# Loading most of w_k in fp32 by the hardware queues, with a newly searched instruction order

## The chip, the cores and the metric

One core of a Trainium2 chip. The metric is the device time of one execution in microseconds (us), as the median of several; lower is better. Two kernels are compared by executions on the same chip, taken in rounds.

## The reference

An attention without softmax, with an RMS norm, feeds a channel-mixing block. There are 8 batches, 8 heads of 64, a sequence of 576, a model width of 512 and a hidden width of 1024.

```python
kv  = einsum('bhsd,bhse->bhde', k, v)
out = einsum('bhsd,bhde->bhse', q, kv)
x   = out / sqrt(mean(out*out) + 1e-6) * g_norm        # then heads are concatenated
xk  = mu_k*x + (1-mu_k)*x_prev ;  xr = mu_r*x + (1-mu_r)*x_prev   # x_prev: one row back
k2  = relu(xk @ w_k) ; r = sigmoid(xr @ w_r)
result = r * ((k2*k2) @ w_v)
```

## The kernel before

The kernel is a set of named pieces (a matmul group, a copy, a load), and one long list, ORDER, says in which order they are emitted. Every engine runs its own pieces in that order, so the list fixes each engine's queue. `qtr0.1` is the transpose of q of batch 0, head pair 1; `kv`, `u`, `ss`, `rr` follow in the attention; `k2.4`, `r2.0`, `v2.0.0` are the matmuls of row group 2 (512 rows); `idle:61` puts 61 filler matmuls on zeros.

```python
def run(self, filler):
    for token in ORDER:
        name, _, eng = token.partition(":")
        if name == "idle":
            filler(int(eng)); continue
        p = self.pieces[name]
        p.fn(eng or p.on[0])
```

Before the change the first head pair of batch 0 comes in fp32 by the SP and ACT queues and is cast on chip. Everything else comes by GpSimd's queue, which casts in flight.

```python
def first_load(n, eng):                      # n in k, v, q
    (nc.sync if eng == "SP" else nc.scalar).dma_start(out=first_view(n), in_=part(n, 0, 0, 2))
...
for i in range(2):                           # w_k in two column halves, cast in flight
    cs = slice(512 * i, 512 * i + 512)
    l = load_w(w_k_sb[:, :, cs], moe_w_k[:, cs], -700 + 0.1 * i, 2.6, f"w_k{i}")
```

From batch 3 on, q is turned by two DMA transposes on SP (`qt6.0` and `qt6.2` in batch 6, one for each two head pairs). A gate on GpSimd reads the first one's result before the next batch is loaded. From batch 5 on the inverse norms make a round trip through DRAM: SP writes them (`ro5`), and two DMAs on GpSimd's queue bring them back, broadcast to 64 partitions each (`rb5`). SP also writes the results (`store...`).

```python
def q_turn(_, hs):
    nc.sync.dma_start_transpose(out=get(qT)[:, hs]..., in_=q2.t[:, hs]...)
...
gate = add({"POOL": 0.3}, lambda _: nc.gpsimd.tensor_copy(out=turned, in_=qT.t[0:1, 0, 0:1]),
           deps=[qtc[0]], bufs=[qT], name=f"gate{b}")
for n in ("k", "v", "q"):
    whole[(n, b + 1)].deps.append(gate)
...
def rms_back(_):
    for e in range(2):
        nc.gpsimd.dma_start(out=get(rs)[64 * e:64 * e + 64],
                            in_=rd.t.rearrange("(i e) c -> e i c", e=2)[e].partition_broadcast(64))
```

Of the kernel before, what the change touches and what calls it, by code (L numbers as in the profile page):

```python
# [15 lines left out]
setup loadq0.2 ident ident9 first_k first_q cast_q:DVE idle:61 qtr0.0 first_v cast_v:DVE cast_k:ACT idle:1 kv0.0  # L16
small qc0.0#2:DVE tr9 qtr0.1 qc0.1#2:DVE qc0.1:DVE qc0.0:ACT edge cols kvc0.0:ACT table u0.0 loadk0.2 loadv0.2 kv0.1
uc0.0:DVE sq0.0 loadq0.6 idle:4 qtr0.3 qc0.3:DVE kvc0.1:ACT u0.1 uc0.1:ACT sq0.1 qc0.3#2:ACT u0.0#2 ss0.0
uc0.0#2:ACT sq0.0#2 gcols rr0.0 mul0.0 d0.0 idle:7 ss0.1 rr0.1 idle:4 ss0.0#2 rr0.0#2 loadq0.4 loadv0.6 loadk0.6
kv0.3 qtr0.2 mul0.1 mul0.0#2 qc0.2#2:ACT kvc0.3:ACT d0.0#2 gk0.0#2:DVE loadv0.4 loadk0.4 idle:6 kv0.2 kvc0.2:ACT  # L20
gk0.1:DVE mr0.1#2:DVE qc0.2:ACT u0.3 uc0.3:ACT sq0.3 idle:7 u0.2 uc0.2:ACT loadq1.0 mt0.0:ACT gk0.0:ACT u0.2#2
uc0.2#2:DVE sq0.2 idle:4 ss0.3 rr0.3 idle:5 ss0.2 rr0.2 sq0.2#2 loadk1.0 loadv1.0 gk0.1#2:DVE idle:1 ss0.2#2 rr0.2#2
xk0.0 d0.1 mr0.1:ACT xk0.1 mul0.3 xk0.1#2 mul0.2 mul0.2#2 gk0.2:DVE gk0.2#2:DVE d0.2#2 idle:11 qtr1.0 qc1.0:ACT
gk0.3:DVE xk0.2 mr0.0:DVE xr0.0 kv1.0 kvc1.0:ACT idle:17 u1.01 u1.00 w_k0 idle:3 k0.a0.1 k0.a0.0 d0.2 xk0.3 k0.a0.2
uc1.01:ACT gk0.3#2:ACT mr0.2:ACT sq1.01 ss1.01 k0.a0.3 rr1.01 relu0.00 xk0.3#2 xk0.2#2 w_k1 idle:6 k0.a1.3 k0.a1.2
uc1.00:DVE d0.3 sq1.00 k0.a1.0 k0.a1.1 relu0.01 ss1.00 mr0.3:DVE xk0.0#2 mr0.2#2:DVE k0.b1 relu0.11 mt0.1:ACT rr1.00
mr0.3#2:DVE ksq0.00 w_r loadv1.4 k0.b0 relu0.10 xr0.2#2 g.w_r:DVE xr0.1 mr0.0#2:DVE mt0.3:DVE xr0.3 xr0.0#2
mt0.2:DVE xr0.2 r0.2 r0.3 sig0.1 g.w_k02:DVE xt0.2 g.w_k12:DVE ksq0.10 loadq1.4 qtr1.2 loadk1.4 qc1.2:DVE kv1.2
kvc1.2:DVE ksq0.11 r0.0 u1.11 uc1.11:ACT u1.10 uc1.10:ACT w_v0 ksq0.01 r0.1 sig0.0 v0.0.0 xt0.0 sq1.11 ss1.11 rr1.11
sq1.10 ss1.10 mul1.0 g.w_k00:DVE v0.2.0 w_v1 v0.2.1 v0.0.1 v0.1.0 v0.3.0 d1.0 xk1.0 rr1.10 mul1.2 d1.2 xk1.2 v0.1.1  # L30
out0.0 store0.0#2 store0.0 g.w_k10:ACT v0.3.1 out0.1 xr1.2 loadq2.0 qtr2.2 qc2.2:ACT qtr2.0 qc2.0:ACT k1.2 k1.3
relu1.1 loadv2.0 loadk2.0 kv2.0 kvc2.0:ACT xr1.0 k1.4 u2.00 u2.11 uc2.11:DVE uc2.00:ACT sq2.00 loadq3.0 ql3.1:DVE
k1.5 relu1.2 u2.01 uc2.01:ACT u2.10 uc2.10:DVE sq2.11 ql3.0:DVE sq2.01 ql3.3:DVE ksq1.1 k1.0 k1.1 relu1.0 ss2.00
rr2.00 k1.6 ss2.01 rr2.01 k1.7 relu1.3 ss2.11 rr2.11 r1.0 ksq1.0 ql3.2:DVE sq2.10 ss2.10 rr2.10 r1.1 sig1.0 r1.2
loadv3.0 loadk3.0 kv3.0 kvc3.0:ACT r1.3 ksq1.2 mul2.0 ksq1.3 v1.0.0 mul2.2 d2.2 xr2.2 qt3.0 u3.00 xk2.2 d2.0 u3.01
uc3.01:ACT sq3.01 uc3.00:ACT sq3.00 sig1.1 xk2.0 qt3.2 v1.0.1 v1.1.0 v1.1.1 out1.0 store1.0#2 xr2.0 ss3.01 rr3.01
ss3.00 rr3.00 v1.2.0 v1.2.1 v1.3.0 v1.3.1 out1.1 gate3 loadq4.0 ql4.2:ACT ql4.0:ACT ql4.1:DVE u3.11 uc3.11:ACT u3.10
mul3.0 uc3.10:ACT ql4.3:DVE k2.4 d3.0 k2.5 relu2.2 ksq2.2 sq3.10 k2.6 k2.7 relu2.3 k2.0 k2.1 relu2.0 sq3.11 ss3.11
ss3.10 rr3.11 k2.2 ksq2.3 rr3.10 mul3.2 k2.3 relu2.1 ksq2.1 r2.0 loadk4.0 loadv4.0 kv4.0 kvc4.0:DVE r2.1 sig2.0
store0.1#2 qt4.0 ksq2.0 u4.01 uc4.01:DVE u4.00 uc4.00:DVE r2.2 r2.3 sig2.1 store0.1 store1.0 xk3.0 sq4.00 qt4.2  # L40
u4.11 uc4.11:DVE u4.10 uc4.10:ACT sq4.10 gate4 loadq5.0 ql5.1:ACT ql5.0:DVE sq4.11 d3.2 xk3.2 v2.2.0 v2.2.1 v2.3.0
ss4.10 ql5.2:ACT v2.0.0 ss4.00 v2.0.1 v2.3.1 out2.1 ql5.3:ACT rr4.10 v2.1.0 ss4.11 xr3.0 v2.1.1 out2.0 rr4.00 rr4.11
mul4.2 k3.0 k3.1 loadv5.0 loadk5.0 kv5.0 relu3.0 kvc5.0:ACT k3.6 xr3.2 qt5.0 gate5 ksq3.0 d4.2 sq4.01 qt5.2 u5.01
u5.00 uc5.01:ACT xk4.2 sq5.01 uc5.00:ACT k3.7 relu3.3 k3.2 u5.11 u5.10 uc5.10:ACT uc5.11:ACT sq5.10 sq5.11 ksq3.3
sq5.00 k3.3 relu3.1 ksq3.1 k3.4 k3.5 relu3.2 ksq3.2 r3.0 ss5 loadq6.0 ql6.2:DVE ql6.3:DVE ql6.0:DVE ql6.1:DVE
store2.1#2 store1.1#2 store2.0 store1.1 rr5 ro5 store2.1 r3.1 ss4.01 rr4.01 mul4.0 d4.0 sig3.0 v3.0.0 v3.0.1 v3.1.0
v3.1.1 out3.0 xr4.0 xk4.0 xr4.2 loadk6.0 loadv6.0 r3.2 r3.3 v3.2.0 v3.2.1 v3.3.0 kv6.0 kvc6.0:DVE v3.3.1 sig3.1
out3.1 k4.4 qt6.0 qt6.2 store3.0#2 store2.0#2 u6.10 u6.01 uc6.01:ACT k4.5 relu4.2 uc6.10:DVE sq6.10 rb5 mul5.0 d5.0
xk5.0 k4.2 k4.3 relu4.1 mul5.2 u6.00 ksq4.2 uc6.00:ACT sq6.00 u6.11 uc6.11:ACT sq6.01 sq6.11 d5.2 xk5.2 ksq4.1 k4.0
k4.1 relu4.0 ksq4.0 r4.0 r4.1 sig4.0 k4.6 ss6 rr6 ro6 gate6 loadk7.0 loadv7.0 kv7.0 loadq7.0 ql7.0:DVE ql7.1:DVE  # L50
qt7.0 store3.0 k4.7 relu4.3 ksq4.3 ql7.3:DVE xr5.2 k5.2 k5.3 ql7.2:ACT relu5.1 rb6 k5.0 k5.1 relu5.0 r4.2 r4.3
v4.2.0 sig4.1 store3.1 v4.2.1 v4.3.0 v4.3.1 store3.1#2 v4.0.0 xr5.0 kvc7.0:DVE u7.01 u7.00 uc7.00:ACT uc7.01:ACT
out4.1 sq7.00 ksq5.1 mul6.0 qt7.2 v4.0.1 v4.1.0 v4.1.1 out4.0 store4.0#2 d6.0 k5.6 k5.7 relu5.3 mul6.2 ksq5.0 sq7.01
u7.11 u7.10 uc7.10:ACT sq7.10 uc7.11:ACT ksq5.3 sq7.11 k5.4 k5.5 relu5.2 ksq5.2 r5.2 r5.3 sig5.1 d6.2 xr6.2 xk6.2
xk6.0 ss7 rr7 store4.1#2 ro7 store4.1 rb7 r5.0 r5.1 v5.0.0 v5.0.1 v5.1.0 v5.1.1 sig5.0 out5.0 store5.0 store5.0#2
store4.0 k6.6 k6.7 relu6.3 k6.2 k6.3 ksq6.3 relu6.1 ksq6.1 xr6.0 k6.0 k6.1 relu6.0 k6.4 k6.5 relu6.2 ksq6.0 mul7.2
ksq6.2 v5.2.0 v5.2.1 v5.3.0 v5.3.1 out5.1 mul7.0 r6.2 r6.3 v6.2.0 sig6.1 v6.2.1 v6.3.0 v6.3.1 d7.0 xr7.0 out6.1 d7.2
xk7.0 store5.1 store6.1#2 store5.1#2 xk7.2 r6.0 r6.1 v6.0.0 v6.0.1 v6.1.0 v6.1.1 sig6.0 out6.0 k8.2 k8.3 relu8.1
ksq8.1 k7.6 k7.7 relu7.3 k8.0 k8.1 relu8.0 ksq8.0 ksq7.3 k8.6 k8.7 relu8.3 k7.0 k7.1 relu7.0 xr7.2 ksq8.3 ksq7.0
k7.4 k7.5 relu7.2 k7.2 k7.3 relu7.1 k8.4 k8.5 relu8.2 ksq7.1 ksq7.2 r7.2 r7.3 v7.2.0 v7.2.1 v7.3.0 v7.3.1 sig7.1  # L60
ksq8.2 out7.1 store6.1 store6.0#2 store7.1#2 store6.0 store7.1 r7.0 r7.1 sig7.0 r8.0 r8.1 sig8.0 v7.0.0 v7.0.1
v7.1.0 v7.1.1 out7.0 v8.0.0 v8.0.1 out8.0 v8.1.0 v8.1.1 out8.0#2 store7.0 store8.0#2 store8.0 store7.0#2 r8.2 r8.3
v8.2.0 sig8.1 v8.2.1 out8.1 store8.1 v8.3.0 v8.3.1 v8.3.0#2 v8.3.1#2 out8.1#2 store8.1#2 out8.1#3 store8.1#3
# [40 lines left out]
def kernel(  # L104
# [125 lines left out]
    first = {n: Buf("out") for n in src}  # L230

    def first_view(n):
        return get(first[n]).rearrange("p a c -> p (a c)")[0:NP, 0:2 * NJ * HD].rearrange("p (h c) -> p h c", h=2)

    def first_load(n, eng):
        def fn(_):
            (nc.sync if eng == "SP" else nc.scalar).dma_start(out=first_view(n), in_=part(n, 0, 0, 2))

        return add({eng: 0.42}, fn, bufs=[first[n]], due=-2000, land=0.8, name="first_" + n)

    firsts = {n: first_load(n, eng) for n, eng in (("k", "SP"), ("v", "ACT"), ("q", "SP"))}
# [31 lines left out]
    def load(b, n, h0, h1, due):  # L273
        def fn(_):
            nc.gpsimd.dma_start(out=get(kvq[(n, b)])[:, h0:h1, :], in_=part(n, b, h0, h1))  # L275

        p = add({"POOL": 0.64 if b == 0 else 0.76}, fn, bufs=[kvq[(n, b)]], due=due, land=(h1 - h0) * (0.37 if b < 3 else 0.43),
                name=f"load{n}{b}.{h0}")
        for h in range(h0, h1):
            loaded[(n, b, h)] = p  # L280
        return p

    whole = {}
    for n in ("k", "v", "q"):
        p = add({"DVE": dve_us(768, 2), "ACT": act_us(768, True)},
                lambda eng, n=n: copy(eng, get(kvq[(n, 0)])[:, 0:2, :], first_view(n)),
                deps=[firsts[n]], bufs=[kvq[(n, 0)], first[n]], name=f"cast_{n}")
        loaded[(n, 0, 0)] = loaded[(n, 0, 1)] = p
    for h0 in (2, 4, 6):
        for i, n in enumerate(("k", "v", "q")):  # L290
            load(0, n, h0, h0 + 2, -900 + 10 * h0 + i)
# [34 lines left out]
    for i in range(2):  # L326
        cs = slice(512 * i, 512 * i + 512)
        l = load_w(w_k_sb[:, :, cs], moe_w_k[:, cs], -700 + 0.1 * i, 2.6, f"w_k{i}")
        p_wk.append([l])
# [627 lines left out]
```

## Time and profile before

| what | before | where |
|---|---|---|
| median time | 203.49 us (203.43 to 204.22) | runs |
| PE busy | 192.6 of 201.7 us, with 12.3 us of fillers | page, parts 1 and 5 |
| second half of k, group 0, starts | 25.12 us | PE timeline |
| PE's listed waits after 35 us | 1.5 us, the largest 0.53 | waits |
| last matmul ends, span ends | 197.5 and 201.7 us | PE timeline |

The prediction below shows the lines. In a timeline line the columns are start, duration, engine, source line, operation, output<-inputs, shapes and count, and in brackets the idle time before it with the name of what ended it. SPq and POOLq stand for what the SP and GpSimd queues issue. Matmul durations in a timeline are modelled ends, so start-to-start times are the safer reading. The granted clock is the share of its full clock that PE was given, as the trace records it.

### The profile page before, as it was taken

How to read it: one execution, taken by the hardware profiler on the slowest of the kernel's cores; microseconds unless marked ns; L12 is line 12 of the kernel's file. 1: busy time of each engine (PE TensorE's matmuls, PEld its weight loads, DVE VectorE, ACT ScalarE, POOL GpSimd, SP SyncE). 2: the span in 40 equal slices, each digit the busy share in tenths (PEclk: the TensorE clock that was granted, in tenths of full speed). 3: DMA queues.
4: the chain of work that ended last, by engine and by line, in shares of the span. 5: the costliest groups of instructions: out<-in, count | busy, mean ns of one | idle time of the engine just before them, and what ended most of it. 6: DMA issues, size and time to landing. Idle time of an engine off the chain costs nothing.

```text
span 201.7 us, 4116 instructions
## 1 busy us (share of the span) xinstructions
PE 192.6 (95%) x1629; PEld 103.4 (51%) x1651; DVE 147.2 (73%) x332; ACT 116.2 (58%) x148; POOL 33.4 (17%) x53
## 2 busy tenths in 40 slices
PE   7999899999999999999999989999999999999991
PEld 7867775454544454543457654444444444444451
DVE  1589988998898959799799985699486854432321
ACT  2588688666978597948723887268452226644020
POOL 7964314000050040040053010000200000000000
PEclk9999999999999999999999999999999999999998
DMA  6999999999969999999999949530742240003263
GB/s 173 200 202 207 204 205 205 204 203 248 171 100 200 217 217 193 173 207 216 207 251 248 203 70 231 156 104 5 185 143 51 66 132 15 2 0 101 69 193 108
DMA packets 39976, 31.69 MB, mean 157 GB/s; under 512 B 13812, under 2 KB 35092, under 8 KB 39956
## 3 DMA queue, kind: packets, MB, share of 16 engines
q0 software_dynamic: 21504, 18.11, 57.0%
q1 hardware_dynamic: 17780, 12.42, 25.9%
q10 hardware_dynamic: 672, 0.89, 1.3%
q8 instruction: 13, 0.21, 0.4%
q14 instruction: 7, 0.06, 0.1%
HBM read 35.33 MB, written 9.46 MB: 222 GB/s over the span
## 4 chain that ended last, share of the span: by engine, by line
PE 74%; DMA 13%; POOL 4%; ACT 3%; issue 2%; SPq 1%; DVE 0%; DVEq 0%; POOLq 0%; ACTq 0%
PE mm L795 25%; PE mm L875 24%; PE mm L853 12%; DMA w_k<-in_moe_w_k_dram 5%; DMA v<-in_v_dram 5%; DMA qT<-q 3%; PE at L649 2%; PE at L567 2%; PE mm L522 2%; PE mm L815 2%; PE mm L892 2%; PE at L892 2%; PE at L701 2%; POOL k L275 1%; POOL q L275 1%
## 5 line engine op out<-in xcount | busy, mean ns | idle before, releaser
L795 PE MATMUL mm<-xk,w_k 128*128 128x512 bf16 (+1 forms) x281 | 58.5, 355 | 0.4
L875 PE MATMUL mm<-w_v,sqk 128*128 128x512 bf16 x251 | 57.8, 379 | 0.6 <-issue 0.3
L799 ACT ACTIVATE relu<-mm 128x1024 bf16<-128x1024 f32 x36 | 36.9, 1024 | 27.1 <-PE mm L795 23.2
L795 PEld LDWEIGHTS <-w_k 128*128 128x128 bf16 x288 | 27.2, 98 | 26.7 <-issue 1.8
L875 PEld LDWEIGHTS <-sqk 128*128 128x128 bf16 x256 | 24.7, 98 | 29.2 <-issue 1.1
L853 PE MATMUL mm<-w_r,xr 128*128 128x512 bf16 x135 | 33.4, 379 | 0.8 <-issue 0.5
L879 DVE TENSOR_TENSOR out<-mm,sig 128x1024 f32<-128x1024 f32 x16 | 19.5, 1223 | 19.8 <-PE mm L875 15.8
L858 ACT ACTIVATE sig<-mm 128x1024 bf16<-128x1024 f32 x18 | 18.4, 1025 | 26.6 <-PE mm L853 26.5
L802 DVE TENSOR_TENSOR sqk<-relu 128x1024 bf16<-128x1024 bf16 x32 | 21.7, 687 | 10.9 <-ACT relu L799 10.7
L853 PEld LDWEIGHTS <-xr 128*128 128x128 bf16 x144 | 13.5, 98 | 15.6 <-issue 0.9
L185 ACT CAST uT<-at 128x576 bf16<-128x576 f32 x21 | 12.6, 641 | 12.2 <-PE at L649 12.2
L743 DVE TENSOR_SCALAR md<-d,cols 128x576 bf16<-128x576 bf16 x56 | 18.4, 371 | 0.3
L194 ACT ACT_TABLE_LOAD x12 | 15.4, 1283 | 0.2
L763 PE MATMUL mm<-zero 128*128 128x128 bf16 x137 | 12.3, 251 | 1.1 <-DVE zero L245 1.1
L717 DVE TENSOR_TENSOR xT<-uT,rs 128x1152 bf16<-128x1152 bf16 x14 | 10.5, 752 | 2.9 <-ACT rs L705 2.8
L656 DVE TENSOR_TENSOR sq<-uT 128x576 bf16<-128x576 bf16 x28 | 12.1, 451 | 0.8 <-ACT uT L185 0.6
L705 ACT ACTIVATE rs<-at,eps 128x576 bf16<-128x576 f32 x16 | 11.2, 738 | 1.8 <-PE at L701 1.7
L763 PEld LDWEIGHTS <-zero 128*128 128x128 bf16 x137 | 10.5, 116 | 2.9 <-issue 1.3
L684 POOL DMA_DIRECT2D rs<-rd x6 | 3.8, 634 | 44.2 <-DVE xk L746 20.6
L746 DVE TENSOR_TENSOR xk<-md,xT 128x1152 bf16<-128x1152 bf16 x14 | 10.6, 759 | 0.5
L746 DVE TENSOR_TENSOR xr<-md,xT 128x1152 bf16<-128x1152 bf16 x14 | 10.6, 759 | 0.5
L729 DVE TENSOR_TENSOR d<-xT 128x1152 bf16<-128x1152 bf16 x14 | 10.5, 753 | 0.2
(89 smaller groups left out, 175.2 us busy)
## 6 DMA issues: line engine op xcount, KB each, us to landing
out_dram<-out SPq DMA_DIRECT2D x22, 192.0 KB, 4.7
q<-in_q_dram POOLq DMA_DIRECT2D x6, 576.0 KB, 10.0
v<-in_v_dram POOLq DMA_DIRECT2D x6, 576.0 KB, 12.6
k<-in_k_dram POOLq DMA_DIRECT2D x6, 576.0 KB, 11.1
out_dram<-out SPq DMA_DIRECT2D x23, 128.0 KB, 2.2
rs<-rd POOLq DMA_DIRECT2D x6, 288.0 KB, 5.6
out_dram<-out SPq DMA_DIRECT2D x22, 64.0 KB, 6.6
w_k<-in_moe_w_k_dram POOLq DMA_DIRECT2D x2, 512.0 KB, 11.5
```

The lines of the kernel that those rows point to most:

```text
L185: nc.scalar.copy(out=dst, in_=src)
L194: nc.scalar.preload_act_table_set(name)
L743: nc.vector.tensor_scalar(out=get(md)[:, hp], in0=d.t[:, hp], scalar1=cols[:, m0 + hp:m0 + hp + 1], scalar2=None, op0=ALU.mult)
L746: nc.vector.tensor_tensor(out=dst[:, hs, c0:c0 + S], in0=md.t[:, hs], in1=xT.t[:, hs, 0:S], op=ALU.add)
L763: nc.tensor.matmul(get(k_ps[i])[:, 0, 0:128], zero[:, 0:128], zero[:, 128:256], start=not k_seen[i], stop=not k_seen[i])
L795: nc.tensor.matmul(get(ps)[:, fc % 2, a0:a1], w_k_sb[:, cc, 128 * fc:128 * fc + 128], xk[:, cc, x0:x0 + a1 - a0], start=(cc == 0), stop=(c ...
L799: nc.scalar.activation(out=get(rt), in_=ps.t, func=AF.Relu)
L802: nc.vector.tensor_mul(out=get(sqk)[:, 2 * f2:2 * f2 + 2, :], in0=rt.t, in1=rt.t)
L853: nc.tensor.matmul(get(ps)[:, ci % 2, :], xr[:, cc, n0:n0 + 128], w_r_sb[:, cc, :], start=(cc == 0), stop=(cc == NHP - 1))
L858: nc.scalar.activation(out=get(sg), in_=ps.t, func=AF.Sigmoid)
L875: nc.tensor.matmul(get(ps)[:, ci % 2, :], sqk.t[:, fc, 128 * ci:128 * ci + 128], w_v_sb[:, fc, :], start=(fc == 0), stop=(fc == NFC - 1))
L879: nc.vector.tensor_mul(out=get(ot)[:, xs, :], in0=ps.t[:, xs, :], in1=sg.t[:, xs, :])
```

## The change

The intent is to have w_k on chip before PE wants it. Three of its four row blocks (512 KB each in fp32) take the fast first place on the SP and ACT queues and are cast on chip. The first head pair goes to GpSimd's queue like the others, and the fourth row block stays there. The order was searched again, all of it, with two of the search's landing estimates raised.

```diff
-    first = {n: Buf("out") for n in src}
+    first = [Buf("out") for _ in range(3)]
-            (nc.sync if eng == "SP" else nc.scalar).dma_start(out=first_view(n), in_=part(n, 0, 0, 2))
+            (nc.sync if eng == "SP" else nc.scalar).dma_start(out=first_view(i), in_=moe_w_k[128 * i:128 * i + 128, :])
-    for h0 in (2, 4, 6):
+    for h0 in (0, 2, 4, 6):
         for i, n in enumerate(("k", "v", "q")):
             load(0, n, h0, h0 + 2, -900 + 10 * h0 + i)
+    p_wk = [add(..., lambda eng, i=i: copy(eng, w_k_sb[:, i, :], first_view(i)), ..., name=f"cast_{i}") for i in range(3)]
+    p_wk.append(add({"POOL": 0.8}, lambda _: nc.gpsimd.dma_start(out=w_k_sb[:, 3, :], in_=moe_w_k[384:512, :]), ...))
-    land=(h1 - h0) * (0.37 if b < 3 else 0.43)
+    land=(h1 - h0) * (0.37 if b < 3 else 0.45)
-    rms_back, deps=[c], bufs=[rd, rs], land=2.2
+    rms_back, deps=[c], bufs=[rd, rs], land=3.2
     ...                      # ORDER: every line differs; the place that matters later:
-    ro5 store2.1 ... qt6.0 qt6.2 store3.0#2 ... rb5 mul5.0
+    ro5 ... store2.0#2 qt6.0 store2.0 qt6.2 ... rb5 mul5.2
```

## The prediction

> **What bounds the kernel now.** I read the page from the top, then the chain that ended last in order of time, then PE's own timeline of the first 26 us, then a table of DMA share by stretches of 1 us, and last PE's waits after 35 us.
>
> ```profile
> span 201.7 us, 4116 instructions
> ...
> PE 192.6 (95%) x1629; PEld 103.4 (51%) x1651; DVE 147.2 (73%) x332; ACT 116.2 (58%) x148; POOL 33.4 (17%) x53
> ...
> PE 74%; DMA 13%; POOL 4%; ACT 3%; issue 2%; SPq 1%; DVE 0%; DVEq 0%; POOLq 0%; ACTq 0%
> ...
> L763 PE MATMUL mm<-zero 128*128 128x128 bf16 x137 | 12.3, 251 | 1.1 <-DVE zero L245 1.1
> ```
>
> PE is the bound, but not all of its 192.6 us is work: the 137 matmuls on L763 are fillers on zeros, which stand where PE has nothing to do in the prologue. After about 25 us PE is dense: its listed waits after 35 us add up to 1.5 us, the largest being 0.53 us for a v load at 116.5 us. So the end is, to about 1 us, the moment when the dense work starts, plus a fixed 172 us of matmuls, plus the last stores (last matmul at about 197.6, end at 201.7). The change acts on the moment when the dense work starts, and the rest is a reordering.
>
> ```profile
> 1.06 5.91 PE L763 MATMUL mm<-zero 128*128 128x128 bf16 x61 [1.06 <-DVE zero L245]
> 6.89 0.45 PE L387 MATMUL a<-ident,q 96*64 96x96 bf16 x12
> ...
> 20.80 1.49 PE L522 MATMUL mm<-xk,w_k 128*128 128x256 bf16 x12 [0.59 <-DMA w_k<-in_moe_w_k_dram]
> ...
> 25.12 1.15 PE L815 MATMUL mm<-xk,w_k 128*128 128x256 bf16 x9
> ```
>
> Fillers run to 6.89 us, when the first q pair has come (fp32) and is cast. L522 is the first half of k of group 0: it waits for w_k until 20.80, though its other input, xk of the first head pairs, is there from about 16.8 us (the first fused multiply ends then). L815, the second half, opens the dense part at about 25.0 us (the weight load says 25.00). This is the wait that the change is after: the chain has 10.92 us of "DMA w_k" from 9.83 to 20.75.
>
> ```profile
> 3.00:4.00 1.00, 1.00 (x12) 1.00 (x10) 0.00 (x0) 0.00 (x0) 1.00 (x3) 1.00 1.07 352
> 4.00:5.00 1.00, 1.00 (x13) 1.00 (x11) 0.00 (x0) 0.15 (x1) 1.00 (x3) 1.00 1.11 263
> ...
> 7.00:8.00 1.00, 1.00 (x27) 0.83 (x26) 0.49 (x2) 0.33 (x1) 0.97 (x2) 1.00 1.31 199
> ```
>
> The last two columns are DMA share and GB/s. At 3 to 4 us only the fp32 loads (SP and ACT queues) run: 352 GB/s. From 5 us on it is the casting loads: 199 to 204 GB/s until 44 us, counted at the bf16 destination, so some 400 GB/s of fp32 source. The DMA is full all through the prologue: what comes first decides everything.
>
> **What the Trainium skill says.** "DMA: Bandwidth & Descriptors", section "SWDGE vs HWDGE vs iDMA": a cast in flight needs the GpSimd path, the other queues only copy, both kinds run on the same 16 engines, which take turns between them. The trace agrees on the first (every load with a cast is on POOL); that the two take turns I must assume for the new overlap, as before they hardly overlap. The same page, "Latency and other measured facts", gives a first byte after 0.6 us (HWDGE) and about 1 us (SWDGE). Here the first SWDGE load is issued at 1.30 us, yet the rate falls from 352 to 263 only at 4 to 5 us and to 208 at 5 to 6: some 3 us. The measurement decides, and it leaves the engines open to fp32 loads for that long. "VectorE: DVE Perf Modes", "The perf-mode tier table", puts an fp32 copy in SBUF at twice the base rate; here the DVE cast of 96x768 takes 556 to 572 ns, which fits (768/2/0.96 = 400 ns, plus a fixed part). "TensorE: Matmul & The Clock Gate", "Wait — 56ns, not 53.3ns?": 128-column matmuls stand 107 ns apart cold and 56 warm. Here the first 61 fillers stand 5.83/61 = 96 ns apart, later ones 55 to 64 (17 in 1.08 us).
>
> **The change part by part.**
>
> *Removed:* three fp32 loads of head pair 0 (3 x 288 KB = 0.88 MB), their casts (ACT 0.83, DVE 0.56 and 0.57 us), and the two casting loads of w_k (2 x 512 KB at the destination).
>
> *Added:* three fp32 loads of 512 KB (1.57 MB), three casts of 128x1024 (from the measured 768-column ones: one DVE, about 0.70 us, two ACT, about 1.05 us each), three more casting loads for head pair 0 (147 kB at the destination each) and one for the last w_k block (262 kB). The scaling of w_k by g, four pieces as before, goes from three on DVE (478 ns) and one on ACT (1147 ns) to one and three: DVE minus 0.96, ACT plus 2.3 us, at 35 to 40 us, where ACT is busy 3.6 of 5 us. Hidden.
>
> *Fillers:* 137 become 133, but 83 instead of 61 stand first. 83 x 96 ns = 7.9, so the first transposes come at about 9.0 us instead of 6.89. The other 50 at 57 ns make 2.85 us. In all 10.8 us against 5.83 + 76 x 0.057 = 10.2: plus 0.6 us of filler.
>
> *When things land.* The fp32 loads have the engines alone from 1.3 to about 4.4 us: some 0.9 MB at up to 352 GB/s. The other 0.67 MB share. If packets alternate, 4 KB fp32 against 768 B casting (4096 B at 352/16 GB/s is 186 ns, the other 79 ns), fp32 gets about 250 GB/s and is in at about 7 us, with 125 kB of casting loads beside it. From there casting bytes run at 200 GB/s. Completion trails the running sum, in the kernel before, by about 0.8 us early and 1.5 us late (w_k0 and w_k1 there: sums give 18.6 and 21.2, landings 20.75 and 22.7). So, sum and lag together: q of the first pair 8.1, its k and v 9.5; head pair 0 11.9; all of batch 0 16.7 (before: 12.6); first half of batch 1 21.3; the last w_k block 22.8; w_r 26.6; w_v 32.2 and 34.8. The last three are as before: 5.38 MB of casting bytes behind 1.57 MB of fp32, against 5.72 behind 0.88, end at 33.4 against 33.5. The DMA total is no gain.
>
> *PE to the dense part.* The matmuls before L815 are the same but for the two sums of squares of batch 1, 0.24 us each, which move behind it. Non-filler work by start-to-start times is about 10.9 us before and 10.4 after. With 1.06 at the start and the fillers, 22.2 us before (25.0 measured, so 2.8 of waits) and 22.3 after, plus its waits. What it must wait for: the last w_k block at 22.8, then 0.44 each for the last block's two pieces, 0.37 for u of batch 1, 0.44 for the last piece: 24.5 us. By the other path, batch 0 complete at 16.7, kv, u, copy, square, sum, rsqrt, multiply, blend (0.38+0.2+0.85+0.36+0.3+0.6+0.42+0.3, then 0.9 for the other multiply and 0.48) give the last head pair's xk at 21.9, and six more DVE pieces before the second halves are ready: 24.7. So L815 starts at about 24.7 instead of 25.0, 0.3 us earlier, and pays 0.48 us for the two moved sums: plus 0.2 us.
>
> *Later.* The one large wait, 0.53 us at 116.5 (v of batch 7), follows a gate, two stores in front of the transposes on SP (0.51 and 0.59 us in the chain) and a load of 10.54 us. The new order puts more PE work in front of that kv, so I count minus 0.5. A longer assumed landing for the broadcast of the norms and for the loads says that the search now plans with slower DMA, so I take another minus 0.2 for small waits. Sum: 203.5 + 0.2 - 0.5 - 0.2 = 203.0.
>
> **Rivals.**
>
> *Freed w_k:* if w_k was the only brake, xk being ready at 16.8, then 20.8 - 17 = 3.8 us is to be had, time about 199.7. Against: head pairs now come 2 to 4 us later, the fillers are not fewer in time, and the last w_k block still comes by the slow path at 22.8.
>
> *Turned wait:* head pair 1 starves beside the fp32 loads, batch 0 lands 2 us later than I think, and DVE, busy 5.00 of 5.00 us at 15 to 20 already, becomes the path into L815. Time about 205. For it: DVE's share. Against: the casts cost DVE 0.4 us less than before.
>
> *Nothing but the new order:* the prologue is a wash and only the schedule's luck counts, 202.5 to 204. Close to my own view.
>
> **Range and chances.** PE's 172 us of dense work doesn't change, so 2% (4.07 us) would need all of the first rival. I put 203.0, with 201.5 to 204.9 for eight in ten: below, some 40% of what the first rival would bring (1.5 of 3.8 us); above, a prologue later by 1.9 us, nearly the second rival. Faster by 2%: 0.03; slower by 2%: 0.03.
>
> **What would show it.** First transposes at 8.5 to 9.5 us; k0's first matmuls (L522's successor) between 17 and 19 us without a wait for w_k; a wait of PE for the last w_k block, or for xk, at 21 to 23; the second half starting at 24.2 to 25.2; fewer than 1.5 us of listed waits after 35 us. I am wrong if the second half starts before 23.5 (first rival) or after 26 (second), or if PE after 45 us is longer or shorter by more than 1 us.

## The result, and the profile after

The changed kernel took 209.41 us in the median (208.37, 208.78, 210.04 and 211.78) against 203.49. The ratio of its fast runs to the fast runs of before is 1.0266, with a 95% interval of 1.0205 to 1.0326. A ratio here is the mean of one kernel's fast runs over the mean of the other's in the same rounds, so not quite the ratio of the medians. Executions over 1.5% slower than the fastest of the same kernel are left out of the means. The profiled execution was the slowest one, 211.78 us, 1.6% above the fastest, and so it counts as a slow run. I use it for the mechanism. Its sum below accounts for that one execution and is not the size of the change; the size is the ratio of the fast runs, some 5.4 us. The two fastest runs, 208.37 and 208.78 us, had a mean granted clock of 0.992 against 0.979, so they lost less to the clock.

The page after, busy time and chain by engine, and the granted clock by slice of 5.2 us:

```profile
span 209.9 us, 4114 instructions
...
PE 196.1 (93%) x1626; PEld 104.5 (50%) x1647; DVE 148.0 (70%) x326; ACT 116.3 (55%) x151; POOL 34.1 (16%) x55
...
PEclk9999999999999999999997699999999999999998
...
PE 56%; DMA 33%; POOL 2%; issue 2%; SPq 2%; ACT 2%; DVE 1%; POOLq 0%; ACTq 0%
```

The span is 8.2 us longer, PE's share of the chain has fallen from 74% to 56%, and DMA's has risen from 13% to 33%. The clock row has a dip in slices 22 and 23, which was not there before.

The start, from PE's timeline of the changed kernel:

```profile
8.40 0.45 PE L384 MATMUL a<-ident,q 96*64 96x96 bf16 x12
...
16.62 0.38 PE L368 MATMUL a<-v,k 96*64 96x64 bf16 x12
...
21.45 0.57 PE L564 MATMUL at<-v,k 96*64 96x64 bf16 x24
...
24.34 1.91 PE L812 MATMUL mm<-xk,w_k 128*128 128x256 bf16 x16
```

The first transposes, the last kv of batch 0, the first kv of batch 1 and the second half of k of group 0 stand at 8.40, 16.62, 21.45 and 24.34 us. The last one was at 25.12 before. So the start is 0.8 us faster, and the loss comes later. PE's waits after 25 us name the places:

```profile
PE at L646 <- DMA qT<-q: 4.1, 1, 4.1
PE at L564 <- DMA v<-in_v_dram: 1.3, 2, 0.9
PE at L564 <- DMA k<-in_k_dram: 0.9, 1, 0.9
```

One wait of 4.1 us, for a transposed q, is larger than all of PE's waits of before together. This is the same stretch of PE's timeline, before (L649 is u, the matmul on qT):

```profile
106.55 1.04 PE L795 MATMUL mm<-xk,w_k 128*128 128x256 bf16 x8
107.59 0.44 PE L649 MATMUL at<-qT,kv 64*64 64x288 bf16 x8
107.96 2.79 PE L795 MATMUL mm<-xk,w_k 128*128 128x256 bf16 x24
```

and after (the same pieces, L792 and L646):

```profile
108.61 1.04 PE L792 MATMUL mm<-xk,w_k 128*128 128x256 bf16 x8
113.73 0.69 PE L646 MATMUL at<-qT,kv 64*64 64x288 bf16 x8 [4.08 <-DMA qT<-q]
114.35 5.14 PE L792 MATMUL mm<-xk,w_k 128*128 128x256 bf16 x24
```

PE stands still for 4.08 us, and then the 24 matmuls that took 2.79 us take 5.14. The table of stretches for the changed kernel shows why; the columns after the length are busy time and count of PE, PEld, DVE, ACT and POOL, then PEclk, DMA share and GB/s:

```profile
110.00:111.00 1.00, 0.00 (x0) 0.00 (x0) 0.96 (x4) 0.00 (x0) 0.00 (x0) 1.00 1.00 104
...
112.00:113.00 1.00, 0.00 (x0) 0.00 (x0) 0.00 (x0) 0.00 (x0) 0.00 (x0) 0.68 1.41 182
113.00:114.00 1.00, 0.27 (x8) 0.18 (x7) 0.00 (x0) 0.00 (x0) 0.00 (x0) 0.50 1.30 198
```

The granted clock falls to one half at about 112.4 us. The trace's clock record holds it there for 6.83 us, to about 119.2, and PE works in 5.5 us of that.

**The account of the profiled execution.** PE's listed waits after 25 us, without "issue" and with the 0.51 us at the tail, come to 6.8 us against 0.7 before. Half of 5.5 us at half clock is 2.7. The start gives back 0.78, less 0.48 (the prediction's estimate) for two sums of squares that moved behind it. The sum is 6.1 + 2.7 - 0.3 = 8.5 us; 211.78 - 203.43 = 8.35 was measured.

Why was the transpose late? SP's queue and GpSimd's queue, before, are:

```profile
97.37 1.15 SPq L774 DMA_DIRECT2D out_dram<-out  x2
98.69 4.72 SPq L603 DMA_TRANSPOSE qT<-q  x2
103.51 2.33 SPq L774 DMA_DIRECT2D out_dram<-out  x4
```

```profile
101.83 1.26 POOL L684 DMA_DIRECT2D rs<-rd  x2 [10.89 <-DMA rd<-rc]
104.16 0.60 POOL L612 COPY turned<-qT 1x1 bf16<-1x1 bf16 x1 [1.07 <-DMA qT<-q]
```

and SP's queue after is:

```profile
99.73 1.54 SPq L600 DMA_TRANSPOSE qT<-q  x1
101.32 1.64 SPq L771 DMA_DIRECT2D out_dram<-out  x2
103.05 2.19 SPq L600 DMA_TRANSPOSE qT<-q  x1
```

and GpSimd's queue after:

```profile
103.21 1.26 POOL L681 DMA_DIRECT2D rs<-rd  x2 [9.59 <-DMA rd<-rc]
```

Before, both transposes of batch 6 go one behind the other. After, a store stands between them, so the second starts to issue at 103.05 us. The broadcast of the norms of batch 5 (`rs<-rd`) is issued at 103.21 us. The chain of the changed kernel has "103.05 10.63 DMA qT<-q": 10.6 us from issue to landing. (Experiment 2 shows the same transpose, issued behind the same store, land in 4.5 us.) The packet records of the two traces (my count, by packet size, in steps of 1 us) show what happened on the engines. A transpose has 1152 packets of 256 B. Before, they ran at 733 and 1018 in a microsecond and were all but done when the 4608 B packets of the broadcast began. After, the first 694 of the second transpose went through within a microsecond. Then the broadcast began, and the rest came at 144, 197, 88 and 29. The 4 B packets, which I take for the reports of the transpose's end, came last, from 111.3 to 112.8 us. The broadcast suffers as well: issue to landing was 5.7 to 6.1 us before and 9.7 to 10.4 after.

Theory A is thus that the new order lets the second transpose run into the broadcast. Theory B is that the gate, which waits for the first transpose alone, lets the loads of batch 7 in beside the second. Theory C is that the new start shifts all later DMA and thereby makes the loss.

### The profile page after: what moved, and what is told of

Same layout as the page of the kernel before. It is cut to its first block, busy times and chain, and to the rows that moved or that the text cites. A ratio compares the mean times of both kernels' runs of the same rounds, so it can differ in the third digit from the quotient of the medians.

```text
span 209.9 us, 4114 instructions
## 1 busy us (share of the span) xinstructions
PE 196.1 (93%) x1626; PEld 104.5 (50%) x1647; DVE 148.0 (70%) x326; ACT 116.3 (55%) x151; POOL 34.1 (16%) x55
## 4 chain that ended last, share of the span: by engine, by line
PE 56%; DMA 33%; POOL 2%; issue 2%; SPq 2%; ACT 2%; DVE 1%; POOLq 0%; ACTq 0%
PE mm L792 19%; PE mm L870 15%; DMA qT<-q 12%; DMA v<-in_v_dram 11%; DMA q<-in_q_dram 10%; PE mm L848 9%; PE mm L519 2%; PE at L887 2%; PE mm L812 2%; PE mm L887 2%; PE at L564 1%; PE at L646 1%; SPq L771 1%; POOL k L276 1%; SPq L600 1%
## 5 line engine op out<-in xcount | busy, mean ns | idle before, releaser
L792 PE MATMUL mm<-xk,w_k 128*128 128x512 bf16 (+1 forms) x282 | 61.1, 367 | 0.4
L792 PEld LDWEIGHTS <-w_k 128*128 128x128 bf16 x288 | 28.6, 102 | 27.9 <-issue 2.0
L853 ACT ACTIVATE sig<-mm 128x1024 bf16<-128x1024 f32 x18 | 18.4, 1023 | 21.3 <-PE mm L848 21.2
L186 ACT CAST uT<-at 128x576 bf16<-128x576 f32 x16 | 9.9, 639 | 12.4 <-PE at L646 12.2
L743 DVE TENSOR_TENSOR xr<-md,xT 128x1152 bf16<-128x1152 bf16 x14 | 10.6, 759 | 0.5
L743 DVE TENSOR_TENSOR xk<-md,xT 128x1152 bf16<-128x1152 bf16 x14 | 10.6, 759 | 0.5
L188 DVE CAST uT<-at 128x576 bf16<-128x576 f32 x12 | 8.9, 753 | 2.9 <-PE at L646 2.8
```

The lines of the kernel that those rows point to most:

```text
L743: nc.vector.tensor_tensor(out=dst[:, hs, c0:c0 + S], in0=md.t[:, hs], in1=xT.t[:, hs, 0:S], op=ALU.add)
L792: nc.tensor.matmul(get(ps)[:, fc % 2, a0:a1], w_k_sb[:, cc, 128 * fc:128 * fc + 128], xk[:, cc, x0:x0 + a1 - a0], start=(cc == 0), stop=(c ...
L853: nc.scalar.activation(out=get(sg), in_=ps.t, func=AF.Sigmoid)
```

## The experiments

All twelve kernels gave correct results. All edits of ORDER are shown by their tokens.

**1. The transposes one behind the other.**

```diff
-store2.0#2 qt6.0 store2.0 qt6.2
+store2.0#2 qt6.0 qt6.2 store2.0
```

> The changed kernel with one pair of tokens swapped on SP: the second transpose of batch 6 directly behind the first, the stores of group 2 (first half) after both. Theory A (the second transpose, issued 3.3 us after the first because two stores stand between, meets the broadcast of the norms of batch 5 on the same DMA engines, and PE waits 4.1 us and then runs at half clock): the wait of PE for qT goes from 4.1 us to under 1 us, and the time from about 208.6 to 203.0-204.8. Theory B (the gate that waits for the first transpose alone lets the loads of batch 7 in beside the second): the gate opens as before, so most of the wait stays, time above 206.5. Theory C (the new start shifts all later DMA): no change, 208-210.

Measured: 203.76, 204.28, 207.39 and 209.84 us, with the kernel before at 203.58 to 205.19. The ratio of the fast runs is 0.9988 (0.9937 to 1.004). In the profiled run (204.28) PE has no wait for qT:

```profile
108.90 0.44 PE L645 MATMUL at<-qT,kv 64*64 64x288 bf16 x8
109.27 2.79 PE L791 MATMUL mm<-xk,w_k 128*128 128x256 bf16 x24
```

The wait and the half clock are gone together: 2.79 us again for the 24 matmuls. One token moved took away the loss in the fast runs, as Theory A said, but only two of the four runs lie in its band. The two runs at 207 and 210 count as slow and have no trace. That the collision came back in them is plausible but not shown: in the profiled run the data of the second transpose was through at 105.7 us, the broadcast began at 105.6, and the 4 B packets at the end came at 107 to 108, with u due at 108.9. The margin was about 1 us.

**2. The broadcast held back.**

```diff
-... k4.3 rb5 mul5.2 ... relu4.0 gate6 loadq7.0
+... k4.3 gate6 rb5 mul5.2 ... relu4.0 loadq7.0
```

> The changed kernel with the gate of batch 6 moved ahead of the broadcast of the norms on the GpSimd queue, so that the broadcast is issued only after the first transpose has landed; the stores still stand between the two transposes. Theory A: the second transpose has 2 to 3 us more of the engines to itself, PE's wait for it falls from 4.1 us to under 2 us, and the time to 203.5-206 (the norms come later and may cost some of it). Theory B: the loads of batch 7 come as early as before, wait and time stay, above 207.5. Theory C: no change.

Measured: 205.25 to 206.79 us, ratio 1.008 (1.0036 to 1.0123). There is no listed wait for qT and the mid-run clock stays full. SP's and GpSimd's queues show the store in its place and the hold:

```profile
102.36 2.25 SPq L599 DMA_TRANSPOSE qT<-q  x1
```

```profile
105.30 0.18 POOL L608 COPY turned<-qT 1x1 bf16<-1x1 bf16 x1 [12.08 <-DMA qT<-q]
105.87 0.65 POOL L680 DMA_DIRECT2D rs<-rd  x1 [0.40 <-issue]
...
107.30 0.79 POOL L275 DMA_DIRECT2D q<-in_q_dram  x1
```

The store still stands between the transposes, the second is issued at 102.36 us, and yet it lands in time, 4.5 us later. The loads of batch 7 are issued at 107.30, near their time in the changed kernel (107.18). So it was the broadcast that the transpose met first; experiment 3 asks about the loads alone. The norms come later, and PE pays 0.6 us for xk and 0.4 for a relu, which it did not before.

**3. The loads of batch 7 held back instead.**

```diff
-tensor_copy(out=turned, in_=qT.t[0:1, 0, 0:1]),                  deps=[qtc[0]]
+tensor_copy(out=turned, in_=qT.t[0:1, 2 if b == 6 else 0, 0:1]), deps=[qtc[2 if b == 6 else 0]]
```

> The changed kernel with the gate of batch 6 waiting for the second transpose in place of the first; order unchanged. Theory A: the loads of batch 7 stand behind the broadcast in the same queue and have moved nothing while the transpose was slow, so PE's wait for qT stays at 3.5 to 4.5 us, and as the loads then come some 5 us later the kv of batch 7 waits too: 208-213. Theory B: the wait falls under 1.5 us and the time to 205 or less. Theory C: no change or worse.

Measured: 208.32, 209.24, 210.88 and 211.35 us, ratio 1.0305 (1.0243 to 1.0368). PE's timeline in the profiled run:

```profile
112.41 0.44 PE L645 MATMUL at<-qT,kv 64*64 64x288 bf16 x8 [3.55 <-DMA qT<-q]
112.78 2.79 PE L791 MATMUL mm<-xk,w_k 128*128 128x256 bf16 x24
```

With the loads out of the way until 112.8 us the wait is still 3.55 us. Theory B falls. This run also gives the wait without the half clock: 208.32 us. Its listed waits (3.5 + 0.9 + 0.5 + 0.4) exceed those of before by 4.6 us, and its time that of the profiled run of before (203.43) by 4.9. Why the clock stayed full here is taken up in the last section.

**4. New loads and start, old order for the rest.** ORDER is the changed kernel's up to `k0.b0`, then the kernel before's list without what has been emitted.

> The changed kernel's loads and its order up to the second half of k of group 0 (about 28 us), and the order of the kernel before for all that is left. Theories A and B (the loss comes from the order after 50 us): 202.7-204.0, within 0.5% of the kernel before. Theory C: the loss stays, above 206.

Measured: 202.79 us once, and 206.41, 206.66 and 206.84. The three count as slow, and one run is left, so there is no ratio. This contradicts what A expected, and three runs lie where C put them. The trace (206.41) shows the same place, though:

```profile
109.50 0.44 PE L645 MATMUL at<-qT,kv 64*64 64x288 bf16 x8 [2.00 <-DMA qT<-q]
109.87 4.46 PE L791 MATMUL mm<-xk,w_k 128*128 128x256 bf16 x24
```

In this order the transposes are adjacent, and they were issued at 98.59 and 100.66 us, as before. On my count their data was through at 105.8 us, just as the broadcast began (105.6), but the 4 B packets that report the end came only at 108.1, when the broadcast was done, and the landing is at 109.5. The collision is thus there in a weaker form, with only the report caught in it: 2.00 us of wait, then 3.41 us at half clock. In this run the start part of the change brings the old order to the edge too. The run at 202.79 lies below all runs of before, but it is a single run and has no trace: what this version is worth without the collision is not shown.

**5. Old start, new order for the rest.** The reverse of 4.

> The kernel before's loads and its order up to the second half of k of group 0, then the changed kernel's order. Theory A (the loss comes with the new order after 50 us, by the second transpose of batch 6 running into the norms' broadcast): PE waits 3 to 4.5 us for qT near 110 us, time 207.5-211. Theory C (the new start, with its other loads, shifts the DMA and thus makes the collision): the wait is under 1 us, time below 205.

Measured: 208.02, 210.87, 211.76 and 213.4 us, ratio 1.027 (1.0177 to 1.0363). The clock halves for 6.83 us, and PE waits for qT as in the changed kernel:

```profile
PE at L649 <- DMA qT<-q: 4.6, 1, 4.6
```

The new order loses by itself, without the new loads, and the ratio is that of the whole change, though two of the runs count as slow and the verdict at 2% is unclear, as the interval begins at 1.0177. Theory C is not needed for the loss.

**6. Both cures.** Experiment 1's swap, and 2's hold with the gate on the second transpose.

> The changed kernel with both cures: the transposes of batch 6 one behind the other, and the broadcast issued only after the gate, which here waits for the second transpose. Theory A: no wait of PE for qT in any execution, so also no run in the 207s and 209s as with the pair alone: all runs 203.0-204.8. If the runs still spread up to 207 and more, something other than this collision makes the slow executions.

Measured: 205.02, 205.43, 205.93 and 206.0 us, ratio 1.0081 (1.0045 to 1.0117). No run reached 207, so the large spread is gone, but the level is 1.2 us above the expected band's upper end at worst. The hold costs more than I thought: PE waits 1.2 us for a v and 0.4 us behind a relu.

**7. Experiment 4 with the hold.**

> New loads and start, the old order for the rest, and the broadcast held until the second transpose has landed. Theory A: the two-valued times of the same kernel without the hold (202.8 once, 206.4 to 206.8 three times) become one value near the lower, 202.5-203.4, about 0.3% under the kernel before. If the 206s stay, the hold was not the cure and the collision not the cause of them.

Measured: 208.52 to 211.39 us, ratio 1.028 (1.0221 to 1.0339). I was wrong. There is no wait for qT any more, but:

```profile
119.35 1.04 PE L667 MATMUL at<-sq,sel 128*32 128x288 bf16 x8 [3.37 <-DVE sq L652]
121.50 1.49 PE L563 MATMUL at<-v,k 96*64 96x64 bf16 x48 [1.11 <-DMA v<-in_v_dram]
```

In the old order the multiply by the norms of batch 5 stands ahead of the squares of batch 6 in DVE's queue. Held norms hold DVE (it sat idle for 4.61 us for them), and PE waits for the squares; behind that the clock halves for 6.83 us. The wait has only moved, so this run is no test of what the collision cost in experiment 4.

**8. The hold alone, on the kernel before.**

> The kernel before with nothing but the hold: the gate of batch 6 waits for the second transpose and stands before the broadcast. Theory A: there the transposes end just as the broadcast starts, so the hold changes little: 203.0-204.0, with less spread. Rival: the hold costs time by itself, as the norms and the loads of batch 7 come later: 204.5-206.

Measured: 204.52 us, and 207.36, 207.46 and 207.53; ratio 1.0137 (1.0064 to 1.0209). The verdict at 2% is unclear, but the rival was right that the hold costs time by itself; three runs lie above even its band, and they have no trace. The hold is evidence about the cause, in 2, and not a cure.

**9. The loads alone.** The changed loads in the order of before, token by token; `w_k1` goes, and the casts stand where the old ones stood.

```diff
-setup loadq0.2 ident ident9 first_k first_q cast_q:DVE idle:61 qtr0.0 first_v cast_v:DVE cast_k:ACT idle:1 kv0.0
+setup loadq0.0 ident ident9 first_0 first_1 idle:61 loadk0.0 loadv0.0 loadq0.2 first_2 cast_1:ACT cast_0:DVE cast_2:ACT qtr0.0 idle:1 kv0.0
```

> The change of the loads alone: three row blocks of w_k by fp32 loads with casts on chip, head pair 0 by casting loads, one casting load for the last w_k block, and otherwise the order of the kernel before, token by token (no new search). My prediction's view (the prologue is a wash): the first transposes come 1.5 to 2.5 us later than before, the second half of k of group 0 starts within 1.2 us of 25.1 us, time 203.5-205.5 if no collision at 105-110 us follows, 206-210 if the small shift brings it about. Rival (the loads free the start): the second half starts before 23.5 us and the time is 202 or less.

Measured: 206.28, 206.6, 208.32 and 209.41 us, ratio 1.0162 (1.0096 to 1.0227), a verdict of unclear at 2%. The second half of k of group 0 starts at 28.68 us, 3.6 us later than before and beyond both expectations. The stretches show what goes with it:

```profile
8.00:10.00 2.00, 1.20 (x26) 1.03 (x27) 0.26 (x1) 0.74 (x3) 1.66 (x3) 0.81 1.31 199
...
14.00:16.00 2.00, 2.00 (x18) 1.56 (x15) 1.31 (x6) 1.75 (x5) 1.02 (x2) 0.50 1.31 198
```

PE waited 1.05 us for the first q at 7.9 and 0.80 us for the first v at 9.35, and the clock was at one half for 6.83 us from 9.25 us on. The times lie in the band that I had given for a collision, but PE's wait for qT is only 0.6 us here: the loss is one of the start. In the changed kernel, with 83 fillers in place of 61, the clock stayed full in the prologue. That the fillers did this is not shown, and experiment 10, with the same start, lost the clock in the prologue all the same.

**10. Experiment 4 with the transposes earlier on SP.**

```diff
-rr5 ro5 store2.1 ... qt6.0 qt6.2 store3.0#2
+rr5 ro5 qt6.0 qt6.2 store2.1 ... store3.0#2
```

> New loads and start, old order for the rest, but the two transposes of batch 6 directly behind the store of the norms on SP, ahead of the store of group 2 that took 1.15 us of SP. Theory A: the transposes are through before the broadcast begins, PE's wait for qT (2.0 us in that order without this) is gone, and the runs fall together near the one good run of it: 202.3-203.3. If they stay at 206-207, the margin is not set by SP.

Measured: 204.51 to 206.51 us, ratio 1.0077 (1.0021 to 1.0134). This sits between the two predictions. In the profiled run SP's norms were written at 98.52 us, 1.9 us later than in 4; the clock had been at one half for 3.41 us in the prologue of that execution, which fits. The transposes were thus issued at 99.62, not earlier, and PE waited 0.9 us for qT and 1.0 us for a multiply. In that run another event took the margin. It does not explain the rest: the two runs at 204.51 and 204.62 us had a granted clock of 1.0 and 0.998 and still lie 1.2 us above Theory A's band, and they have no trace. The test settles nothing about the margin.

**11. The same move in the kernel before.**

> The kernel before with the same one move (the transposes of batch 6 ahead of the store of group 2). Theory A: it was on the good side of the collision in most executions already, so 203.0-203.7, as before or 0.2% less. Rival: transposes that come earlier slow the loads of batch 6 or the store and cost 0.5 us or more.

Measured: 203.64 to 205.35 us, ratio 1.0057 (1.0007 to 1.0106). There is no wait for qT. PE waits 0.6 us for a multiply of the output, which it did not before. The move is no gain where the collision does not happen, and the rival, a cost of 0.5 us or more, came nearer than my 203.0 to 203.7.

**12. The changed kernel mended in four places.**

```diff
-store2.0#2 qt6.0 store2.0 qt6.2
+qt6.0 qt6.2 store2.0#2 store2.0
-r1.2 kv3.0 r1.3
+r1.2 r1.3 kv3.0
-kv5.0 relu3.1 k3.0
+relu3.1 k3.0 kv5.0
-v8.3.0 v8.3.1 out8.1#2 v8.3.0#2 v8.3.1#2 out8.1#3
+v8.3.0 v8.3.1 v8.3.0#2 v8.3.1#2 out8.1#2 out8.1#3
```

> The changed kernel with four edits of its order: both transposes of batch 6 ahead of both stores; the kv of batch 3 one r piece later (PE waited 0.9 us there for v); the kv of batch 5 one k piece later (0.6 to 0.9 us for k); the last half matmuls not behind the first half's multiply (0.5 us). If the collision and these three waits are the whole loss, the time is that of the pair-swapped kernel's good runs (203.8-204.3) less some 1.5 us, 202.0-203.3, and the spread is small. If it stays at 204 or more, the waits were not on the path, or return further on.

Measured: 203.73, 203.76, 204.47 and 205.28 us, ratio 1.0026 (0.9977 to 1.0076): the same as before, and not below it as I had hoped. PE's waits in the profiled run (203.76) are:

```profile
PE at L645 <- DVE kv L187: 0.5, 1, 0.5
PE mm L791 <- DVE out L873: 0.4, 1, 0.4
```

The waits for qT, v, k and the tail are gone. Two of them returned in part: where the kv of batch 5 moved back, u now waits 0.5 us for its copy, and a k piece waits 0.4 us for the output multiply. With the order repaired in four places the change as a whole is worth nothing measurable. No version that I ran beats both kernels by more than the noise.

## Why the prediction was wrong

It said 203.0 us, 201.5 to 204.9, with 3% for slower by 2%. The measured median is 209.41 and the ratio 1.027, so the number, the range and the class were all wrong.

**The start: right.** I had the first transposes at about 9.0 us and got 8.40; batch 0 complete at 16.7, and its last kv ran at 16.62; the first half of batch 1 at 21.3, and its kv at 21.45; the second half of k at 24.7, and it came at 24.34. The net of the start was put at plus 0.2 us; by PE's timelines it is minus 0.3 (0.78 earlier, 0.48 for the moved sums). Of the rivals, "Freed w_k" and "Turned wait" were rejected rightly. Of the signs named, k0 began at 17.93 us without a wait for w_k, as it said. The wait for the last w_k block or for xk at 21 to 23 us is not in the list, and 8.40 lies just under the 8.5 to 9.5 named: the 96 ns per filler was a mean of some 107 ns until 5.97 us and 56 after, and most of the added fillers ran at 56. Two slips changed nothing: the pieces listed after 16.7 add up to 21.5, not 21.9, and the casting loads ran at 193 to 215 GB/s between 5 and 44 us, not 199 to 204. One assumption inside failed without harm. I let the fp32 and casting loads take turns from 4.4 us on. In fact the fp32 loads ran almost alone, as a table of stretches shows in the changed kernel:

```profile
3.00:4.00 1.00, 1.00 (x12) 1.00 (x11) 0.00 (x0) 0.00 (x0) 1.00 (x3) 1.00 1.05 426
...
5.00:6.00 1.00, 1.00 (x12) 1.00 (x11) 0.00 (x0) 0.00 (x0) 1.00 (x2) 1.00 1.03 408
```

They moved 408 to 426 GB/s, not 352, and were through by about 6.5 us.

**The step that failed is "Later".** It said: "The new order puts more PE work in front of that kv, so I count minus 0.5", and "another minus 0.2 for small waits". The fast runs put 5 to 6 us of loss there in the place of a gain of 0.7. The error behind it is in the first part: "a fixed 172 us of matmuls". From the second half of k to the last matmul it was 172.4 us before and 182.0 in the profiled run after. I took PE's density after 25 us as a property of the work, while it was a property of one order. A new order over the same work had to earn it again, on all queues. The rival "Nothing but the new order" had the place right and the size wrong. I looked only at PE's tokens around the known waits and did not go through SP's and GpSimd's queues of the new order. The pair `qt6.0 store2.0 qt6.2` stood in the diff. The chain before had the transposes as a link of 5.35 us on the path, and I read its two stores in front of the transposes as a delay to be removed, not as a warning that this link had no slack.

**What stood in its place.** In the profiled run, 4.08 us of wait for the second transpose, 2.7 us lost to the half clock that followed, and 2.7 us of smaller waits (v of batches 3 and 6, k of batch 5, the tail), against 0.7 us of waits, elsewhere, before. Experiments 1, 2, 3 and 5 show the first two: the loss goes when the transposes are adjacent or the broadcast waits, stays when the loads wait, and is there without the new loads. Experiment 12 shows that the rest goes when its three places are repaired, though 0.9 us returns elsewhere.

**"What would show it" did its work.** It named "PE after 45 us is longer or shorter by more than 1 us" as proof against me, and that is what happened. "Fewer than 1.5 us of listed waits after 35 us" was missed by a factor of nearly five (7.3 us).

**Left open.** Theory C is not dead: in experiment 4 the new start with the old order collided in the profiled run, and two more took as long without a trace. Which small shift of the loads of batch 6 did it is not shown. Neither is the cause of the two slow runs of experiment 1. The kernel before is not safe either: one of its eight runs beside experiments 5 to 8 took 210.19 us at a granted clock of 0.979, like the changed kernel's slowest, and has no trace. That the search put a store between the transposes because its model has no sharing between DMA queues is a guess from its single landing times.

## What to carry to other kernels

When a change comes with a new order for everything, the order is the larger part of the change: go through each queue of it, the DMA queues first, and not only through the engine that is the bound. Two DMAs can each take about double when they meet (here 10.6 us against 4.5, and 9.7 to 10.4 against 5.7 to 6.1), so a link on the critical chain that just clears another transfer is a place to protect in any reordering. A stall of PE is to be priced with the half clock that can follow it: here 4.1 us of wait cost nearly 7, while 3.55 us in experiment 3 cost no clock at all, so part of this price is luck.

## What the Trainium skill lacked or had wrong

- "TensorE: Matmul & The Clock Gate", section "What's actually happening", gives the slow clock after at least one idle window of about 3.4 us, in free-running windows. The windows agree: in every trace here the changes of the clock lie whole multiples of 3.413 us apart. What no page says is how idle a window has to be. I cut PE's timelines at these multiples (my count, with modelled matmul times). After 100 us the clock halved behind windows in which PE was busy for 0.20 (changed kernel), 0.41 (experiment 4), 0.40 (5) and 0.27 (7) of the time, and not behind 0.50 and 0.46 (experiment 3). So the length of a wait does not decide by itself: 2.00 us inside one window halved the clock, and 3.55 us, split 1.7 to 1.8 over two, did not. In the prologue, with its small matmuls, busy time does not sort the cases: the clock halved behind 0.49 (experiment 9) and 0.67 (10), and not behind 0.67 (4).
- No page that I read has what a DMA transpose loses beside a broadcast to 64 partitions. Here the 256 B packets fell from as many as 1018 in a microsecond to between 29 and 197, the transpose took 10.6 us from issue to landing against 4.5 with the broadcast held (experiment 2), and the broadcast 9.7 to 10.4 us against 5.7 to 6.1 before. Even a transpose whose data was through can wait: its report stood 2.3 us behind the broadcast (experiment 4, 105.8 to 108.1 us).
- "DMA: Bandwidth & Descriptors", section "Latency and other measured facts", has about 1 us for the first byte of a casting load. In the changed kernel the first was issued at 1.30 us, and DMA still ran at the fp32 loads' 408 GB/s between 5 and 6 us, with 8 casting packets on my count. Whether they were late or stood behind the fp32 packets is not shown.
